# A 2:4-pruned linear layer on one core: one weight copy split over two DMA queues, four products moved back, one magnitude pass halved

## The chip, the core and the metric

The kernel runs on one core of one Trainium2 chip. The metric is the device time of one execution in microseconds (us). The median of three runs is given; lower is better. A separate execution was recorded by the hardware profiler, and the profile below is of that one.

The engines that matter here are TensorE (PE in the profile; PEld is its weight load), VectorE (DVE), ScalarE (ACT) and SyncE (SP). SP and ACT also issue DMA transfers, each on a queue of its own; the transfers of both are carried by the same 16 DMA engines.

## The reference, cut to what matters

```python
B, S, D = 16, 512, 1024              # x: B,S,D   w: D,D   b: D   all bf16
wg = w.reshape(D // 4, 4, D)         # groups of four neighbouring rows
mag = jnp.abs(wg)
order = jnp.argsort(mag, 1)
thr = jnp.take_along_axis(mag, order[:, 2:3, :], 1)
mask = mag >= thr                    # the two largest of each four stay
wp = (wg * mask).reshape(D, D)
return jnp.einsum("bsd,df->bsf", x, wp) + b
```

So the kernel prunes a 1024 x 1024 weight, multiplies 8192 tokens by it and adds a bias.

## The kernel before, in words

The 8192 tokens are 64 tiles of 128. From tile 9 on, the work is a plain loop (line 301): for each tile, 16 matmuls of 512 columns against the pruned weight in natural row order (`wp_nat`, one tensor for each half h of the columns), with the transposed x brought by DMA transposes in batches (`issue_batch`, line 219: tiles 9 to 11, then 12 to 15, then eight at a time). VectorE adds the bias out of PSUM, and ACT's queue stores.

The first nine tiles are computed while the weight is still arriving and being pruned. That part is a list of tokens written out by hand, `FRONT`; each engine does its share of it in the list's order. `w` comes in packed order: the four rows of a group lie in one partition. It is cut in seven pieces, numbered as in `pieces`: 0 to 3 are the first 512 contraction rows (g = 0) in four steps of 256 columns, 4 and 5 are columns 0 to 511 of the second 512 rows (g = 1), and 6 is the last 512 columns of g = 1. The tokens:

- `A.i` takes the magnitudes of piece i (line 122 on VectorE for pieces 0 and 1, line 120 on ScalarE for the others); `P.i` finds the threshold, the mask, and multiplies the weight by it in place (lines 133 to 143, VectorE).
- `W`, `w`: warm-up matmuls on zeros. `T.t` transposes the first half of x tile t on TensorE (line 160), `C.t` copies it out on ScalarE (line 165).
- `M.i.t` multiplies tile t by piece i, four matmuls (line 179), one for each of m = 0 to 3; `X.q.t` does so for a whole quarter of 512 columns; `N.i.t.m` does the one matmul m.
- `V.h.t` copies the partial sum of g = 0 to SBUF on ScalarE (line 193), and `O.h.t` adds the partial sum of g = 1 to it on VectorE (line 197).
- `U.g.h.c0.c1` moves a pruned piece to natural rows (line 150): four DMAs, j = 0 to 3, each writes one block of 128 rows of `wp_nat`. The products with g = 1 (pieces 4 to 6) read these blocks, m being the block j.
- `L.k` issues the k-th batch of transposes of x (line 219).

`U` and `L` are issued by SP, in the order of the list; a queue's next issue waits until the one before it is issued. ACT's own loads, two of them, come at the very start (the second half of piece 0's rows and x tiles 2 and 3); after the last `V` it issues nothing until the stores. Every DMA reports its landing on one of eight semaphores, used in turn, and before one is used again the issuing queue waits for the landing of the DMA that had it last.

Around the places that are changed, the list before runs like this:

```
A.0 P.0 W ... T.0 T.1 C.0 T.2 T.3 C.1 w T.4 T.5 C.2 w M.0.0 A.1 C.3 M.0.1 P.1 C.4 T.6 T.7 C.5
M.0.2 M.0.3 C.6 M.0.4 A.2 M.0.5 M.0.6 C.7 P.2 M.1.0 A.3 M.0.7 M.1.1 A.4 M.1.2 M.1.3 V.0.0
...
P.6 U.1.1.0.512 U.0.1.0.512 L.0 L.1 L.2 V.1.2 X.1.8 ... V.1.8 M.4.6 ... M.5.7 O.0.4 X.2.8 O.0.5
N.6.0.0 N.6.0.1 O.0.6 N.6.0.2 N.6.1.0 N.6.1.1 O.0.7 N.6.0.3 N.6.1.2 N.6.1.3 M.6.2 ...
```

`U.1.1.0.512` is piece 6; its four blocks are called j0 to j3 below. `N.6.0.0` is the first product that reads j0, `N.6.0.1` j1, `N.6.0.2` j2 and `N.6.0.3` j3.

Of the kernel before, what the change touches and what calls it, by code (L numbers as in the profile page):

```python
# [10 lines left out]
def kernel(  # L11
# [7 lines left out]
    nc = tc.nc  # L19
    P = 128  # L20
    bf16 = mybir.dt.bfloat16
    fp32 = mybir.dt.float32
    u16 = mybir.dt.uint16
    Alu = mybir.AluOpType
    Act = mybir.ActivationFunctionType
    K = tc.keep_in_program_order
# [36 lines left out]
    w_gh = {(g, h): const.tile([P, 4, FH], bf16, name=f"w_{g}_{h}") for g in range(2) for h in range(2)}  # L63

    def w_of(i):
        g, c0, c1 = pieces[i]
        return w_gh[(g, c0 // FH)][:, :, c0 % FH:c0 % FH + c1 - c0]
# [39 lines left out]
    def warm(n):  # L107
        K(nc.tensor.matmul(bank[7][:, :n], lhsT=zeros[:, :P], rhs=zeros[:, :n], start=True, stop=True))  # L108
# [3 lines left out]
    def abs_piece(i, on_act):  # L112
        g, c0, c1 = pieces[i]
        n = c1 - c0
        if n <= 256:
            mag = mags_pool.tile([P, 4, n], bf16, name="mag")[:]
        else:
            mag = const.tile([P, 4, n], bf16, name=f"mag_{i}")[:]
        if on_act:
            K(nc.scalar.activation(mag, w_of(i), Act.Abs))  # L120
        else:
            K(nc.vector.tensor_single_scalar(
                mag.bitcast(u16), w_of(i).bitcast(u16), 0x7FFF, op=Alu.bitwise_and))
        mags[i] = mag

    def prep_piece(i):
        g, c0, c1 = pieces[i]
        n = c1 - c0
        mag = mags.pop(i)
        magv = mag.rearrange("p (a j) f -> p a j f", j=2)  # L130
        hi = tmp.tile([P, 2, FH], bf16, name="hi")[:, :, :n]
        lo = tmp.tile([P, 2, FH], bf16, name="lo")[:, :, :n]
        K(nc.vector.tensor_tensor(hi, magv[:, :, 0, :], magv[:, :, 1, :], op=Alu.max))  # L133
        K(nc.vector.tensor_tensor(lo, magv[:, :, 0, :], magv[:, :, 1, :], op=Alu.min))  # L134
        t1 = tmp.tile([P, FH], bf16, name="t1")[:, :n]
        t2 = tmp.tile([P, FH], bf16, name="t2")[:, :n]
        K(nc.vector.tensor_tensor(t1, hi[:, 0, :], hi[:, 1, :], op=Alu.min))
        K(nc.vector.tensor_tensor(t2, lo[:, 0, :], lo[:, 1, :], op=Alu.max))
        thr = tmp.tile([P, FH], bf16, name="thr")[:, :n]
        K(nc.vector.tensor_tensor(thr, t1, t2, op=Alu.max))  # L140
        mask = tmp.tile([P, 4, FH], bf16, name="mask")[:, :, :n]
        K(nc.vector.tensor_tensor(mask, mag, thr[:, None, :].to_broadcast([P, 4, n]), op=Alu.is_ge))  # L142
        K(nc.vector.tensor_tensor(w_of(i), w_of(i), mask, op=Alu.mult))  # L143

    wp_nat = [const.tile([P, KT, FH], bf16, name=f"wp_nat{h}") for h in range(2)]


    def unpack(g, h, c0, c1):
        for j in range(4):
            K(nc.sync.dma_start(wp_nat[h][:, 4 * g + j, c0:c1], w_gh[(g, h)][32 * j:32 * (j + 1), :, c0:c1]))  # L150

    xT = {}
    own = {}
# [1 line left out]
    def transpose_half(t):  # L155
        own[(0, t)] = next_bank()
        xv = xh[t].rearrange("p (q m) -> p m q", m=4)
        dst = bank[own[(0, t)]][:].bitcast(bf16)[:, :4 * P].rearrange("p (m q) -> p m q", m=4)
        for m in range(4):
            K(nc.tensor.transpose(dst[:, m, :], xv[:, m, :], ident[:]))  # L160

    def copy_half(t):
        xt = const.tile([P, 4, P], bf16, name=f"xT_{t}")
        src = bank[own[(0, t)]][:].bitcast(bf16)[:, :4 * P].rearrange("p (m q) -> p m q", m=4)
        K(nc.scalar.copy(xt[:], src))  # L165
        xT[t] = xt


    def mm_part(q, t, c0, c1, ms=range(4)):
        g, h = divmod(q, 2)  # L170
        if c0 == 0 and q > 0 and 0 in ms:
            own[(q, t)] = next_bank()
        dst = bank[own[(q, t)]][:, c0:c1]
        for m in ms:
            if g == 0:
                lhs, rhs = xT[t][:, m, :], w_gh[(0, h)][:, m, c0:c1]
            else:
                lhs, rhs = xg1[:, m, t * P:(t + 1) * P], wp_nat[h][:, 4 + m, c0:c1]
            K(nc.tensor.matmul(dst, lhsT=lhs, rhs=rhs, start=c0 == 0 and m == 0, stop=c1 == FH and m == 3))  # L179
# [11 lines left out]
    def to_stage(h, t):  # L191
        stage[(h, t)] = const.tile([P, FH], fp32, name=f"stage{h}_{t}")
        K(nc.scalar.copy(stage[(h, t)][:], bank[own[(h, t)]][:]))  # L193

    def add_stage(h, t):
        st = stage[(h, t)][:]
        K(nc.vector.tensor_tensor(st, bank[own[(2 + h, t)]][:], st, op=Alu.add))  # L197

    def add_bias(h, t):
        f = slice(h * FH, (h + 1) * FH)  # L200
        K(nc.vector.tensor_tensor(get_o(t)[:, f], stage.pop((h, t))[:], bias_sb[:, f], op=Alu.add))  # L201
        if (1 - h, t) not in stage:
            store(t)
# [10 lines left out]
    def issue_batch(t0, nb):  # L214
        if nb < 8:
            xt = const.tile([P, KT, nb * P], bf16, name=f"xTs{t0}")
        else:
            xt = xtb.tile([P, KT, nb * P], bf16, name="xTb")
        K(nc.sync.dma_start_transpose(out=xt[:], in_=xf[t0 * P:(t0 + nb) * P, :]))
        for j in range(nb):  # L220
            xN[t0 + j] = xt[:, :, j * P:(j + 1) * P]
# [8 lines left out]

    FRONT = """
        A.0 P.0 W W W W W W W W w w T.0 T.1 C.0 T.2 T.3 C.1 w T.4 T.5 C.2 w M.0.0 A.1 C.3 M.0.1 P.1 C.4 T.6 T.7 C.5
        M.0.2 M.0.3 C.6 M.0.4 A.2 M.0.5 M.0.6 C.7 P.2 M.1.0 A.3 M.0.7 M.1.1 A.4 M.1.2 M.1.3 V.0.0 M.1.4 M.1.5 V.0.1
        P.3 M.1.6 V.0.2 M.1.7 V.0.3 T.8 M.2.0 C.8 M.2.1 M.2.2 V.0.4 X.0.8 V.0.5 P.4 U.1.0.0.256 V.0.6 M.2.3 M.2.4
        A.5 M.2.5 M.3.0 V.0.7 M.3.1 V.0.8 M.2.6 P.5 U.1.0.256.512 U.0.0.0.512 M.3.2 V.1.0 M.2.7 A.6 M.3.3 M.3.4
        M.3.5 M.3.6 V.1.1 M.3.7 P.6 U.1.1.0.512 U.0.1.0.512 L.0 L.1 L.2 V.1.2 X.1.8 V.1.3 M.4.0 V.1.4 M.4.1 V.1.5
        M.4.2 M.4.3 V.1.6 M.4.4 V.1.7 M.4.5 N.5.0.0 V.1.8 M.4.6 N.5.0.1 N.5.0.2 M.4.7 N.5.0.3 M.5.1 O.0.0 M.5.2
        O.0.1 M.5.3 M.5.4 O.0.2 M.5.5 M.5.6 O.0.3 M.5.7 O.0.4 X.2.8 O.0.5 N.6.0.0 N.6.0.1 O.0.6 N.6.0.2 N.6.1.0
        N.6.1.1 O.0.7 N.6.0.3 N.6.1.2 N.6.1.3 M.6.2 O.0.8 O.1.0 M.6.3 O.1.1 M.6.4 O.1.2 M.6.5 O.1.3 M.6.6 O.1.4
        O.1.5 M.6.7 O.1.6 X.3.8 O.1.7 O.1.8  # L240
    """
    for tok in FRONT.split():
        k, *n = tok.split(".")
        n = [int(c) for c in n]
        if k in "MN":
            g, c0, c1 = pieces[n[0]]
            h = c0 // FH
            mm_part(2 * g + h, n[1], c0 - h * FH, c1 - h * FH, n[2:] or range(4))
        elif k in "Ww":
            warm(FH if k == "W" else P)  # L250
        elif k == "A":
            abs_piece(n[0], n[0] >= 2)
        elif k == "P":
            prep_piece(n[0])
        elif k == "T":
            transpose_half(n[0])
        elif k == "C":
            copy_half(n[0])
        elif k == "X":
            mm_part(n[0], n[1], 0, FH)  # L260
        elif k == "V":
            to_stage(*n)
        elif k == "O":
            add_stage(*n)
        elif k == "B":
            add_bias(*n)
        elif k == "U":
            unpack(*n)
        elif k == "L":
            issue_batch(*batches[n[0]])  # L270
    later = [(h, t) for t in range(T) for h in range(2) if (h, t) in stage]
# [19 lines left out]
    for bi, (t0, nb) in enumerate(batches):  # L291
        if bi >= 1 and bi + 2 < len(batches):
            issue_batch(*batches[bi + 2])
        for t in range(t0, t0 + nb):
# [11 lines left out]
            j = (t - T) % 2  # L306
# [36 lines left out]
```

## Time and profile before

| what | value |
|---|---|
| time, median of 3 runs | 235.18 us (235.05 to 235.23) |
| time of the profiled execution | 234.39 us |
| its span, first to last instruction | 232.6 us |
| TensorE clock granted over the span | 1.000 |
| TensorE busy | 226.6 us, 1163 matmuls recorded |
| VectorE busy | 116.0 us |
| ScalarE busy | 20.7 us |

The profiled execution's time is its span and 1.8 us around it. The rows of the profile are start, duration, engine, line, operation, output<-inputs and count, and in square brackets how long the engine was idle before, with what ended that. A "q" behind an engine's name is its issuing side. A matmul's shown duration is its latency: neighbours overlap, and their cost is the distance between two starts, 0.216 us for 512 columns, 0.109 for 256 and 0.056 for 128. A few matmul records are missing from the trace.

### The profile page before, as it was taken

To read this page: it belongs to the slowest core of one execution; us is meant where nothing else is said; L and a number is where in the kernel's file an instruction comes from. 1 tells how busy PE (TensorE), PEld (TensorE's weight loads), DVE (VectorE), ACT (ScalarE), POOL (GpSimd) and SP (SyncE) were. 2 spreads that over 40 slices of the span, in tenths; PEclk is the share of its full clock that TensorE was granted. 3 is DMA by queue.
4 is the path that set the end of the run, shared out by engine and by line. 5 is a ranking of instruction groups with operands and counts; after the bars stand their busy time and mean duration, and the time that the engine had idled before them with its cause. 6 is when DMAs were issued, how large, how long until landed. Compare 5 with 4: busy or idle time off the path is not lost.

```text
span 232.6 us, 2804 instructions
## 1 busy us (share of the span) xinstructions
PE 226.6 (97%) x1163; PEld 113.8 (49%) x1184; DVE 116.0 (50%) x200; ACT 20.7 (9%) x34; POOL 0.7 (0%) x6
## 2 busy tenths in 40 slices
PE   7999999999999999999999999999999999999995
PEld 3788854444444444444444444444444444444443
DVE  4999898994484234334334324424424423433433
ACT  3999300000000000000000000000000000000000
POOL 1000000000000000000000000000000000000000
PEclk9999999999999999999999999999999999999999
DMA  6993589999998522971259510893229922221132
GB/s 191 353 245 71 124 198 259 194 268 97 293 319 261 208 90 93 269 227 45 90 150 290 191 74 20 217 303 116 90 90 179 272 93 90 90 90 46 47 135 90
DMA packets 77084, 38.19 MB, mean 164 GB/s; under 512 B 62352, under 2 KB 68880, under 8 KB 77072
## 3 DMA queue, kind: packets, MB, share of 16 engines
q1 hardware_dynamic: 67728, 20.91, 42.9%
q10 hardware_dynamic: 9344, 17.11, 20.7%
q8 instruction: 9, 0.15, 0.3%
q14 instruction: 3, 0.02, 0.0%
HBM read 3.54 MB, written 16.78 MB: 87 GB/s over the span
## 4 chain that ended last, share of the span: by engine, by line
PE 94%; DMA 3%; issue 1%; DVE 0%; SPq 0%; DVEq 0%
PE bank L301 80%; PE bank L179 12%; DMA xh<-in_x_dram 2%; PE bank L276 1%; DMA wp_nat<-w 1%; PE bank L160 1%; DVE stage L197 0%; SPq L79 0%; SPq L71 0%; DVE o_sb L286 0%; PE bank L108 0%; SPq L150 0%; DVEq L197 0%
## 5 line engine op out<-in xcount | busy, mean ns | idle before, releaser
L301 PE MATMUL bank<-wp_nat,xTb 128*128 128x512 bf16 x738 | 161.7, 379 | 0.8
L207 DVE TENSOR_TENSOR o_pair<-bank,bias_sb 128x512 bf16<-128x512 f32 x108 | 69.3, 685 | 100.3 <-PE bank L301 95.8
L301 PEld LDWEIGHTS <-xTb 128*128 128x128 bf16 x752 | 73.5, 98 | 88.8
L301 PE MATMUL bank<-wp_nat,xTs 128*128 128x512 bf16 x109 | 24.0, 379 | 0.1
L301 PEld LDWEIGHTS <-xTs 128*128 128x128 bf16 x112 | 11.0, 98 | 13.2
L179 PE MATMUL bank<-w,xT 128*128 128x256 bf16 (+1 forms) x134 | 16.1, 277 | 0.1
L179 PE MATMUL bank<-wp_nat,xg 128*128 128x256 bf16 (+1 forms) x103 | 16.0, 313 | 0.1
L201 DVE TENSOR_TENSOR o_sb<-stage,bias_sb 128x512 bf16<-128x512 f32 x18 | 11.5, 684 | 6.4 <-DMA out_dram<-o_sb 6.4
L179 PEld LDWEIGHTS <-xT 128*128 128x128 bf16 x136 | 13.2, 98 | 2.2
L179 PEld LDWEIGHTS <-xg 128*128 128x128 bf16 x104 | 10.2, 98 | 5.8 <-issue 0.6
L197 DVE TENSOR_TENSOR stage<-bank,stage 128x512 f32<-128x512 f32 x18 | 11.6, 685 | 1.9 <-PE bank L179 1.9
L193 ACT COPY stage<-bank 128x512 f32<-128x512 f32 x18 | 9.2, 614 | 0.0
L120 ACT ACTIVATE mag<-w 128x1024 bf16<-128x1024 bf16 (+1 forms) x5 | 6.1, 1233 | 0.4 <-DMA w<-in_w_dram 0.4
L142 DVE TENSOR_TENSOR mask<-mag,thr 128x1024 bf16<-128x1024 bf16 (+1 forms) x7 | 5.4, 769 | 0.2
L143 DVE TENSOR_TENSOR w<-w,mask 128x1024 bf16<-128x1024 bf16 (+1 forms) x7 | 5.4, 768 | 0.2
L165 ACT COPY xT<-bank 128x512 bf16<-128x512 bf16 x9 | 4.8, 602 | 2.4 <-PE bank L160 2.3
L108 PE MATMUL bank<-zeros 128*128 128x512 bf16 (+1 forms) x12 | 3.7, 456 | 1.2 <-DVE zeros L101 1.2
L276 PE MATMUL bank<-wp_nat,xTb 128*128 128x128 bf16 (+2 forms) x31 | 3.6, 269 | 0.1
L160 PE MATMUL bank<-ident,xh 128*128 128x128 bf16 x36 | 2.8, 222 | 0.7 <-DMA xh<-in_x_dram 0.7
L133 DVE TENSOR_TENSOR hi<-mag 128x512 bf16<-128x512 bf16 (+1 forms) x7 | 3.2, 459 | 0.1
L134 DVE TENSOR_TENSOR lo<-mag 128x512 bf16<-128x512 bf16 (+1 forms) x7 | 3.2, 455 | 0.0
L276 PEld LDWEIGHTS <-xTb 128*128 128x128 bf16 x32 | 2.5, 98 | 1.3
(16 smaller groups left out, 15.3 us busy)
## 6 DMA issues: line engine op xcount, KB each, us to landing
out_dram<-o_pair ACTq DMA_DIRECT2D x26, 512.0 KB, 3.6
out_dram<-o_sb ACTq DMA_DIRECT2D x9, 256.0 KB, 6.3
w<-in_w_dram SPq DMA_DIRECT2D x3, 512.0 KB, 6.5
wp_nat<-w SPq DMA_DIRECT2D x12, 128.0 KB, 2.9
xh<-in_x_dram SPq DMA_DIRECT2D x3, 256.0 KB, 4.6
wp_nat<-w SPq DMA_DIRECT2D x8, 64.0 KB, 2.1
out_dram<-o_pair ACTq DMA_DIRECT2D x2, 256.0 KB, 2.0
xh<-in_x_dram ACTq DMA_DIRECT2D x1, 256.0 KB, 4.2
```

The costliest lines, as they stand in the source:

```text
L120: K(nc.scalar.activation(mag, w_of(i), Act.Abs))
L142: K(nc.vector.tensor_tensor(mask, mag, thr[:, None, :].to_broadcast([P, 4, n]), op=Alu.is_ge))
L143: K(nc.vector.tensor_tensor(w_of(i), w_of(i), mask, op=Alu.mult))
L160: K(nc.tensor.transpose(dst[:, m, :], xv[:, m, :], ident[:]))
L165: K(nc.scalar.copy(xt[:], src))
L179: K(nc.tensor.matmul(dst, lhsT=lhs, rhs=rhs, start=c0 == 0 and m == 0, stop=c1 == FH and m == 3))
L193: K(nc.scalar.copy(stage[(h, t)][:], bank[own[(h, t)]][:]))
L197: K(nc.vector.tensor_tensor(st, bank[own[(2 + h, t)]][:], st, op=Alu.add))
L201: K(nc.vector.tensor_tensor(get_o(t)[:, f], stage.pop((h, t))[:], bias_sb[:, f], op=Alu.add))
L207: K(nc.vector.tensor_tensor(o_sb[:, f], bank[bk][:], bias_sb[:, f], op=Alu.add))
L276: K(nc.tensor.matmul(bank[bk][:, :c1 - c0], lhsT=xN[t][:, kt, :], rhs=wp_nat[h][:, kt, c0:c1], start=kt == 0, stop=kt == KT - 1))
L301: K(nc.tensor.matmul(bank[bks[h]][:], lhsT=xN[t][:, kt, :], rhs=wp_nat[h][:, kt, :], start=kt == 0, stop=kt == KT - 1))
```

## The change

Three things are changed.

1. `abs_piece`: for piece 0 the magnitude pass on VectorE is two instructions, rows m = 0, 1 and rows m = 2, 3, where it was one for all four. The two halves of this piece are loaded by two DMAs, the first on SP's queue and the second on ACT's.
2. `FRONT`: `M.0.7`, the eighth tile's products with piece 0, comes after `M.1.2`; it came after `M.1.0`.
3. `unpack` is given the queue and a range of j. Of piece 6, j0 and j1 stay at their place on SP's queue; j2 and j3 become a token `Z`, issued on ACT's queue, in the list behind `V.1.8`. What followed them on SP's queue (`U.0.1.0.512`, `L.0`, `L.1`, `L.2`) follows j1 directly.

```diff
-            K(nc.vector.tensor_single_scalar(
-                mag.bitcast(u16), w_of(i).bitcast(u16), 0x7FFF, op=Alu.bitwise_and))
+            for ms in (slice(0, 2), slice(2, 4)) if i == 0 else (slice(0, 4),):
+                K(nc.vector.tensor_single_scalar(
+                    mag[:, ms].bitcast(u16), w_of(i)[:, ms].bitcast(u16), 0x7FFF, op=Alu.bitwise_and))
...
-    def unpack(g, h, c0, c1):
-        for j in range(4):
-            K(nc.sync.dma_start(wp_nat[h][:, 4 * g + j, c0:c1], w_gh[(g, h)][32 * j:32 * (j + 1), :, c0:c1]))
+    def unpack(eng, g, h, c0, c1, ja=0, jb=4):
+        for j in range(ja, jb):
+            K(eng.dma_start(wp_nat[h][:, 4 * g + j, c0:c1], w_gh[(g, h)][32 * j:32 * (j + 1), :, c0:c1]))
...
-        M.0.2 M.0.3 C.6 M.0.4 A.2 M.0.5 M.0.6 C.7 P.2 M.1.0 A.3 M.0.7 M.1.1 A.4 M.1.2 M.1.3 V.0.0 M.1.4 M.1.5 V.0.1
+        M.0.2 M.0.3 C.6 M.0.4 A.2 M.0.5 M.0.6 C.7 P.2 M.1.0 A.3 M.1.1 A.4 M.1.2 M.0.7 M.1.3 V.0.0 M.1.4 M.1.5 V.0.1
...
-        M.3.5 M.3.6 V.1.1 M.3.7 P.6 U.1.1.0.512 U.0.1.0.512 L.0 L.1 L.2 V.1.2 X.1.8 V.1.3 M.4.0 V.1.4 M.4.1 V.1.5
-        M.4.2 M.4.3 V.1.6 M.4.4 V.1.7 M.4.5 N.5.0.0 V.1.8 M.4.6 N.5.0.1 N.5.0.2 M.4.7 N.5.0.3 M.5.1 O.0.0 M.5.2
+        M.3.5 M.3.6 V.1.1 M.3.7 P.6 U.1.1.0.512.0.2 U.0.1.0.512 L.0 L.1 L.2 V.1.2 X.1.8 V.1.3 M.4.0 V.1.4 M.4.1
+        V.1.5 M.4.2 M.4.3 V.1.6 M.4.4 V.1.7 M.4.5 N.5.0.0 V.1.8 Z.1.1.0.512.2.4 M.4.6 N.5.0.1 N.5.0.2 M.4.7 N.5.0.3
...
-        elif k == "U":
-            unpack(*n)
+        elif k in "UZ":
+            unpack(nc.sync if k == "U" else nc.scalar, *n)
```

More of the change, by code (lines that the diff above doesn't have):

```diff
@@ L232 @@
         A.0 P.0 W W W W W W W W w w T.0 T.1 C.0 T.2 T.3 C.1 w T.4 T.5 C.2 w M.0.0 A.1 C.3 M.0.1 P.1 C.4 T.6 T.7 C.5
-        M.0.2 M.0.3 C.6 M.0.4 A.2 M.0.5 M.0.6 C.7 P.2 M.1.0 A.3 M.0.7 M.1.1 A.4 M.1.2 M.1.3 V.0.0 M.1.4 M.1.5 V.0.1
+        M.0.2 M.0.3 C.6 M.0.4 A.2 M.0.5 M.0.6 C.7 P.2 M.1.0 A.3 M.1.1 A.4 M.1.2 M.0.7 M.1.3 V.0.0 M.1.4 M.1.5 V.0.1
         P.3 M.1.6 V.0.2 M.1.7 V.0.3 T.8 M.2.0 C.8 M.2.1 M.2.2 V.0.4 X.0.8 V.0.5 P.4 U.1.0.0.256 V.0.6 M.2.3 M.2.4
         A.5 M.2.5 M.3.0 V.0.7 M.3.1 V.0.8 M.2.6 P.5 U.1.0.256.512 U.0.0.0.512 M.3.2 V.1.0 M.2.7 A.6 M.3.3 M.3.4
-        M.3.5 M.3.6 V.1.1 M.3.7 P.6 U.1.1.0.512 U.0.1.0.512 L.0 L.1 L.2 V.1.2 X.1.8 V.1.3 M.4.0 V.1.4 M.4.1 V.1.5
-        M.4.2 M.4.3 V.1.6 M.4.4 V.1.7 M.4.5 N.5.0.0 V.1.8 M.4.6 N.5.0.1 N.5.0.2 M.4.7 N.5.0.3 M.5.1 O.0.0 M.5.2
-        O.0.1 M.5.3 M.5.4 O.0.2 M.5.5 M.5.6 O.0.3 M.5.7 O.0.4 X.2.8 O.0.5 N.6.0.0 N.6.0.1 O.0.6 N.6.0.2 N.6.1.0
-        N.6.1.1 O.0.7 N.6.0.3 N.6.1.2 N.6.1.3 M.6.2 O.0.8 O.1.0 M.6.3 O.1.1 M.6.4 O.1.2 M.6.5 O.1.3 M.6.6 O.1.4
-        O.1.5 M.6.7 O.1.6 X.3.8 O.1.7 O.1.8
+        M.3.5 M.3.6 V.1.1 M.3.7 P.6 U.1.1.0.512.0.2 U.0.1.0.512 L.0 L.1 L.2 V.1.2 X.1.8 V.1.3 M.4.0 V.1.4 M.4.1
+        V.1.5 M.4.2 M.4.3 V.1.6 M.4.4 V.1.7 M.4.5 N.5.0.0 V.1.8 Z.1.1.0.512.2.4 M.4.6 N.5.0.1 N.5.0.2 M.4.7 N.5.0.3
+        M.5.1 O.0.0 M.5.2 O.0.1 M.5.3 M.5.4 O.0.2 M.5.5 M.5.6 O.0.3 M.5.7 O.0.4 X.2.8 O.0.5 N.6.0.0 N.6.0.1 O.0.6
+        N.6.0.2 N.6.1.0 N.6.1.1 O.0.7 N.6.0.3 N.6.1.2 N.6.1.3 M.6.2 O.0.8 O.1.0 M.6.3 O.1.1 M.6.4 O.1.2 M.6.5 O.1.3
+        M.6.6 O.1.4 O.1.5 M.6.7 O.1.6 X.3.8 O.1.7 O.1.8
     """
```

## The prediction, as it was put on record

> **What bounds the kernel now.** I read the page first (busy times, chain by engine), then the chain in order of time, then the timelines of the stretches that the diff touches. All starts below are of the profiled execution.
>
> ```profile
> span 232.6 us, 2804 instructions
> ...
> PE 226.6 (97%) x1163; PEld 113.8 (49%) x1184; DVE 116.0 (50%) x200; ACT 20.7 (9%) x34; POOL 0.7 (0%) x6
> ...
> PE 94%; DMA 3%; issue 1%; DVE 0%; SPq 0%; DVEq 0%
> ```
>
> TensorE is busy for 97% of the span and makes 94% of the chain. The change removes no matmul, so it can only gain TensorE's idle time. Start to start of its matmuls, I find four waits after the first transposes: 0.37 us before 6.38, 0.09 before 6.99, 0.18 before 8.04, 0.03 before 10.73, and then nothing until 31.66. (Other long steps are missing records: two pitches of 0.216.) Two more come at 31.89 and 32.23, and none after that up to the last tile.
>
> ```profile
> 6.25 0.69 DVE L143 TENSOR_TENSOR w<-w,mask 128x1024 bf16<-128x1024 bf16 x1
> ...
> 6.85 0.22 PE L108 MATMUL bank<-zeros 128*128 128x128 bf16 x1
> ...
> 6.99 1.03 PE L179 MATMUL bank<-w,xT 128*128 128x256 bf16 x8
> ...
> 7.27 0.43 DVE L122 TENSOR_SCALAR mag<-w 128x1024 uint16<-128x1024 uint16 x1 [0.33 <-DMA w<-in_w_dram]
> ...
> 8.04 0.48 PEld L160 LDWEIGHTS <-xh 128*128 128x128 bf16 x8 [0.29 <-DMA xh<-in_x_dram]
> ...
> 9.98 0.69 DVE L143 TENSOR_TENSOR w<-w,mask 128x1024 bf16<-128x1024 bf16 x1
> ...
> 10.48 0.57 ACT L165 COPY xT<-bank 128x512 bf16<-128x512 bf16 x1
> ```
>
> This is the timeline of the start. P.0 ends at 6.25 + 0.69 = 6.94 and releases M.0.0 at 6.99. T.6 then waits for x until 8.04, and A.1 for its weight until 7.27: both pinned by a DMA's landing.
>
> ```profile
> 28.56 3.29 DMA wp_nat<-w
> 31.85 0.04 issue
> 31.89 7.84 PE bank L179 x35
> ```
>
> ```profile
> 30.36 1.18 PEld L179 LDWEIGHTS <-xg 128*128 128x128 bf16 x7
> 31.89 0.10 PEld L179 LDWEIGHTS <-xg 128*128 128x128 bf16 x1 [0.35 <-issue]
> 32.23 0.10 PEld L179 LDWEIGHTS <-xg 128*128 128x128 bf16 x1 [0.24 <-issue]
> ```
>
> The chain goes through one DMA of piece 6: j1, issued at 28.56, lands at 31.85, and N.6.0.1 starts at 31.89. N.6.0.0 started at 31.44, so N.6.0.1 was due at 31.66: a wait of 0.24. N.6.0.2 is due at 32.11 and starts at 32.23, behind j2's landing at 32.19: 0.12. Together 0.36 us, 0.15% of the time. That is all that this profile offers the change's third part.
>
> **Part 1, the halved magnitudes.** The loads of piece 0's halves land at 3.29 (SP) and 3.52 (ACT); the one pass starts at 3.54, takes 0.43, and the next step starts at 4.00. No row shows a half pass. It is at least half of the whole, 0.21, and at most the whole, 0.43; two-input rows show 0.42 at 512 elements and 0.28 at 256, so the cost is part fixed: I take 0.29. The first half then runs from 3.31 to 3.60, and the second to about 3.85: 0.14 gained (0 to 0.22, none if the second costs as much as the whole). P.0 ends at 6.80. The warm-up matmul at 6.85 holds TensorE until 6.91, so M.0.0 gains 0.08. M.0.0 and M.0.1 end 0.08 sooner, and T.6 still waits for x until 8.04: worth nothing. If x landed early, the 0.08 would be lost again at M.1.0, which stands at 10.73 behind P.1's end (9.98 + 0.69 = 10.67), and P.1 starts from the landing at 7.27. I take 0.
>
> **Part 2, M.0.7.** Same four matmuls, later. M.0.7 starts at 11.16, and C.7, which it needs, ends at 10.48 + 0.57 = 11.05: it does not wait now, with 0.11 to spare. Behind M.1.1 and M.1.2 it starts 8 x 0.109 = 0.87 later, with 0.98 to spare. M.1.1 and M.1.2 come 0.44 earlier and need only P.1 and copies that are long done. Worth 0 here; up to 0.87 in an execution in which C.7 is late (it stands behind A.2 on ACT, which waits for its weight until 9.52). Nothing is lost: the first V waits behind A.4 until 12.85.
>
> **Part 3, two queues.** On SP, 20 DMAs of line 150 follow each other, then the transposes:
>
> ```profile
> 19.29 13.79 SPq L150 DMA_DIRECT2D wp_nat<-w  x20
> 33.13 7.33 SPq L219 DMA_TRANSPOSE xTs<-in_x_dram  x2
> 40.50 28.76 SPq L219 DMA_TRANSPOSE xTb<-in_x_dram  x2
> ```
>
> ```profile
> wp_nat<-w SPq DMA_DIRECT2D x12, 128.0 KB, 2.9
> ```
>
> They go out every 0.65 us: j0 at 27.96, j1 at 28.56, j2 at 29.21, j3 at 29.86. P.6 is done at 26.97, but SP is still busy with the transfer before until 27.86. ACT's last V ends at 25.29 and its first store goes at 41.69, so Z waits there for P.6 alone, nothing is queued behind it, and j2 goes out at 27.02 and j3 at about 27.6 (an issue took 0.50 on ACT at the start, 0.60 on SP here). With a landing 2.6 to 3.5 us after issue (the rows of this kind) they land between 29.6 and 31.2, before N.6.0.2 can ask: 0.12 gained. j0 and j1 keep their issue times, since what stands ahead of them on SP is unchanged. N.6.0.1 is free of its wait if j1 lands within 3.05 us (2.7 is common, it took 3.29); it keeps 0.24 at 3.29; and it gets worse by as much as j2 and j3 slow it. Ends: 0.36 gained with j1 quick; at the other, j1 later by all of Z's 256 KB at the 200 GB/s that the engines moved from 29 to 34, 1.28 us, less 0.12: 1.16 lost. I take the row itself, 3.29: between 28.5 and 29.5 the engines show a busy share of 0.87, so they have a little room, and from 27.5 to 28.0 they moved only a quarter of that rate, which Z can fill. Sum of part 3: **0.12 us gained.**
>
> What comes later: U.0.1 and the transposes go out 2 x 0.65 = 1.3 us sooner. The batch for tile 16 landed at 62.30 and was used at 63.74; TensorE did not wait for it, so this is worth 0 here.
>
> [...]
>
> **The sum.** 0 + 0 + 0.12. The profiled execution would take 234.39 - 0.12 = 234.27. The median of the runs is 0.79 above that execution; I cannot see where, carry it over as it is, and get 235.18 - 0.12 = 235.06, so 235.05. A difference under about 0.2% (0.47 us) cannot be told from no change.
>
> **The rivals.**
>
> - *The 0.79 us of the usual executions lie in waits that this change shortens.* If C.7 is late by 0.4 more than here, M.0.7 waits 0.3 now and not after; if the batch for tile 16 is late by over its 1.44, the 1.3 us of earlier issue pay for it; and N.6's 0.36 goes. That is 0.5 to 0.8 faster: 234.4 to 234.7. For it: these margins (0.11, 1.44) are thin beside landings that spread by 0.9 us. Against: the profile shows neither wait.
> - *The two queues share the DMA engines, and j0 and j1 pay.* TensorE needs j0 and j1 first, and Z's bytes are ahead of them. From the point where j1 lands 0.59 us later than now (32.44), the loss passes 0.47: with 0.6 to 1.28 us of delay, 235.7 to 236.35. For it: busy share 0.87. Against: Z starts nearly one microsecond ahead, in a half-idle stretch.
> - *Z does not go out early.* A DMA that uses a semaphore again waits for the one eight before it: the store at 62.37 goes right after the batch's landing at 62.30. In the source, Z's j2 is the eighth behind j1. Were they counted so, Z would go at 31.9, land at 34.6, and N.6.0.2 would wait 2.4: 237.6. Against: in the trace semaphores are handed out in the order in which work gets ready (ACT's first load has the first, though SP's stands first in the source); by that order the ones Z takes were free at 26.2.
>
> **How the numbers follow.** The forecast, anything from the full 0.36 gained to 0.45 lost (234.8 to 235.6), gets 0.45; the late waits 0.32; the shared engines 0.20; the late Z 0.03. So faster 0.32, same 0.45, slower 0.23. The range reaches into both neighbours, 234.4 to 235.9, and leaves out the late Z, the upper half of the shared engines and a little of the first rival.
>
> **What would show it.** After: the first magnitude row near 3.3 and P.0's end near 6.80, with T.6 still at its landing; M.0.7 without a wait; two ACT issues of line 150 near 27.0; the transposes near 31.8; N.6.0.2 right behind N.6.0.1. It is wrong if j1 lands after 32.4, if ACT issues Z after 28, or if TensorE's waits before 11 us shrink by over 0.2 us.

## The result, and the profile after

The kernel after takes 235.93 us (median of 19 runs, 234.17 to 236.68); the kernel before, 234.83 (19 runs, 234.32 to 236.08). The ratio is 1.0038, with a 95% interval of 1.0021 to 1.0055: it is slower, by about 0.9 us by the ratio and 1.1 by the medians. The forecast was 0.12 us faster.

The first view is TensorE's weight loads around N.6 in the profile of after (start, duration, engine, line, operation, inputs, count, and the idle time ahead with what ended it).

```profile
32.00 0.31 PEld L180 LDWEIGHTS <-xg 128*128 128x128 bf16 x2
33.95 0.33 PEld L180 LDWEIGHTS <-xg 128*128 128x128 bf16 x3 [1.64 <-DMA wp_nat<-w]
```

The last matmul of X.2.8 starts at 32.43, so N.6.0.0 is due at 32.65; it starts at 33.95. That is one wait of 1.31 us, where before had 0.24 and 0.12. It is for j0, which lands at 33.91. Behind it N.6.0.1 and N.6.0.2 follow without a gap. The chain of the same profile names something else:

```profile
32.06 1.89 DVE stage L198 x3
33.95 0.00 issue
33.95 7.94 PE bank L180 x36
```

A wait for several semaphores is put down to the one that came last. VectorE's addition ended at 33.95 too, but what N.6.0.0 needs of VectorE is the bank of an earlier tile, which was read by 30.3. The weight load's row, and the landing, name the real cause. Where they disagree, ask which data the instruction reads.

Then the issues of `unpack` in the stretch of piece 6 (median landing at the end of the row), and the two queues in order of time:

```profile
wp_nat<-w SPq DMA_DIRECT2D x4, 128.0 KB, 4.1
wp_nat<-w ACTq DMA_DIRECT2D x2, 128.0 KB, 4.3
```

```profile
28.21 1.33 ACTq L151 DMA_DIRECT2D wp_nat<-w  x2
```

ACT issues Z at 28.21, when P.6 ends at 28.18, as forecast. But the transfers that took 2.9 us on one queue now take 4.1 to 4.3: j0 goes out at 28.99 and lands 4.92 later.

This execution had a second difference. x tiles 6 and 7 landed at 9.21 and not at 8.00, so everything from there to N.6 stands 1.2 us later than in the profile of before. The profiled execution took 236.53 us, 0.6 above the median of the runs. The span is 234.7 against 232.6: 1.2 from there, 0.95 from N.6. From the start of tile 9 on, the two profiles agree within 0.02 us: tile 16 starts 24.17 later in both, and the end comes 168.83 after that. Whatever the change does, it has done by tile 9.

### The profile page after: what moved, and what is told of

It reads as the page before. It is cut to its first block, busy times and chain, and to the rows that moved or that the text cites. A ratio compares the mean times of both kernels' runs of the same rounds, so it can differ in the third digit from the quotient of the medians.

```text
span 234.7 us, 2826 instructions
## 1 busy us (share of the span) xinstructions
PE 228.4 (97%) x1184; PEld 114.2 (49%) x1184; DVE 116.4 (50%) x201; ACT 20.8 (9%) x34; POOL 0.7 (0%) x6
## 4 chain that ended last, share of the span: by engine, by line
PE 94%; DMA 3%; DVE 1%; SPq 1%; issue 0%; DVEq 0%
PE bank L302 79%; PE bank L180 13%; DMA xh<-in_x_dram 3%; PE bank L277 1%; DVE stage L198 1%; SPq L71 0%; SPq L79 0%; PE bank L161 0%; DVE o_sb L287 0%; DVEq L198 0%
## 5 line engine op out<-in xcount | busy, mean ns | idle before, releaser
L302 PEld LDWEIGHTS <-xTb 128*128 128x128 bf16 x752 | 73.6, 98 | 88.7
L108 PE MATMUL bank<-zeros 128*128 128x512 bf16 (+1 forms) x12 | 4.2, 509 | 1.2 <-DVE zeros L101 1.2
L161 PEld LDWEIGHTS <-xh 128*128 128x128 bf16 x36 | 2.6, 122 | 1.9 <-DMA xh<-in_x_dram 1.8
```

Of the source, the lines that this page charges most:

```text
L302: K(nc.tensor.matmul(bank[bks[h]][:], lhsT=xN[t][:, kt, :], rhs=wp_nat[h][:, kt, :], start=kt == 0, stop=kt == KT - 1))
```

## The experiments

Each ratio below is to the kernel before, run again beside that group of experiments, with its 95% interval in brackets.

**Which part it is.** The first kernel is before with part 3 alone (`unpack` as in part 3, here and wherever a kernel below splits a piece); the second is after without part 3.

```diff
-P.6 U.1.1.0.512 U.0.1.0.512 ... V.1.8 M.4.6
+P.6 U.1.1.0.512.0.2 U.0.1.0.512 ... V.1.8 Z.1.1.0.512.2.4 M.4.6     (all of the first kernel)
```

> The kernel before with part 3 alone: j2 and j3 of piece 6 on ACT's queue, nothing else changed. Theory A (the two queues share the DMA engines, and j0, which TensorE needs first, lands late behind the bytes of j2 and j3): the whole loss is here, 0.5 to 1.3 us over before, with one TensorE wait of about 1.3 us ahead of N.6.0.0 and j0 landing 4 to 5 us after its issue. Theory B (the loss sits in the first 12 us, with the halved magnitudes or the moved products): within 0.3 us of before, j0 landing under 3.3 us after its issue.

> The kernel after without part 3: halved magnitudes and moved products, all four blocks of piece 6 on SP's queue. Theory A: within 0.3 us of before, the waits at N.6.0.1 and N.6.0.2 together 0.2 to 0.6 us. Theory B: 0.5 to 1.3 us slower than before, with longer TensorE waits before 12 us.

Part 3 alone: 235.68 us, ratio 1.0052 (1.0032 to 1.0072). Without part 3: 234.51, ratio 0.9996 (0.9981 to 1.0011). In the first, j0 lands 4.76 us after its issue and N.6.0.0 waits 1.44; in the second, j0 and j1 land after 2.66 and 2.92, and the only wait is 0.17 at N.6.0.2. The loss is all in part 3, and theory B falls. x tiles 6 and 7 landed at 8.08 and 7.93 in these two. The chain of part 3 alone names the transfer, j0, itself:

```profile
28.14 4.76 DMA wp_nat<-w
32.89 0.05 issue
32.94 7.94 PE bank L179 x36
```

The halved magnitudes do what the forecast said. In the kernel without part 3:

```profile
3.30 0.50 DVE L123 TENSOR_SCALAR mag<-w 128x512 uint16<-128x512 uint16 x2 [2.17 <-DMA w<-in_w_dram]
3.83 0.43 DVE L134 TENSOR_TENSOR hi<-mag 128x512 bf16<-128x512 bf16 x1
```

A half takes 0.29, and the second half runs from 3.51 to the next step at 3.83: 0.32 where the whole took 0.46, so 0.14 is gained, and A.1 still starts at 7.25.

**Bytes, or their order?** Next, the same two queues with j0 and j1 on ACT's; and one queue, with two blocks of U.0.0 moved behind piece 6.

```diff
-P.6 U.1.1.0.512.0.2 ... V.1.8 Z.1.1.0.512.2.4
+P.6 U.1.1.0.512.2.4 ... V.1.8 Z.1.1.0.512.0.2                       (exchange, from part 3 alone)
...
-U.1.0.256.512 U.0.0.0.512 ... P.6 U.1.1.0.512 U.0.1.0.512
+U.1.0.256.512 U.0.0.0.512.0.2 ... P.6 U.1.1.0.512 U.0.0.0.512.2.4 U.0.1.0.512     (from before)
```

> Part 3 the other way round: j0 and j1 on ACT's queue, j2 and j3 on SP's. Theory A (the engines move some 200 GB/s whatever the number of queues, and what is queued first lands first): j0 lands 3.8 us after its issue as Z's j2 did, about when it is due, j1 1.5 us later, so one wait of 0.6 to 1.0 us at N.6.0.1; 0.2 to 0.6 us slower than before, faster than part 3 alone. Rival A2 (only the order matters, the bytes do not): no wait at all, 0.3 us faster than before.

> The kernel before with one queue, but the last two blocks of U.0.0 put behind piece 6 on SP, so that SP is free when P.6 ends: j0 goes out 0.9 us sooner, with two blocks less ahead of it. Theory A: j0 to j3 land 2.6 to 3.3 us after issue, all before they are due, both waits of N.6 are gone, 0.3 to 0.4 us faster than before. If something other than the bytes ahead holds piece 6 (its issue, P.6's end), the waits stay and the time is that of before within 0.2 us.

The exchange: 234.39 us, ratio 0.9993 (0.9981 to 1.0005), and no wait at N.6 at all. Theory A, as I had it, falls. It expected the same 256 KB more among the same transfers to cost 0.6 to 1.0 us, but here everything landed within 2.8 to 3.6 us, also j2 and j3, which come last. Rival A2 (only the order matters) fits this run; the turned exchange below decides against it. Piece 6 ahead: 234.08 us, ratio 0.9979 (0.9968 to 0.9989), no wait at N.6 either; this one came as expected. TensorE's weight loads across N.6, in the exchange and then with piece 6 ahead, show no idle time:

```profile
30.53 3.77 PEld L179 LDWEIGHTS <-xg 128*128 128x128 bf16 x19
```

```profile
30.54 3.88 PEld L179 LDWEIGHTS <-xg 128*128 128x128 bf16 x19
```

The rates tell it. These are windows of 28.5 to 31 us; the last column is GB/s, the one before it the DMA engines' busy share. First before, then part 3 alone, then the exchange:

```profile
28.50:31.00 2.50, 2.46 (x22) 2.06 (x21) 2.50 (x5) 0.00 (x0) 0.00 (x0) 1.00 0.86 202
```

```profile
28.50:31.00 2.50, 2.50 (x24) 2.11 (x22) 2.50 (x6) 0.00 (x0) 0.00 (x0) 1.00 0.94 171
```

```profile
28.50:31.00 2.50, 2.50 (x25) 2.15 (x23) 2.50 (x5) 0.00 (x0) 0.00 (x0) 1.00 0.94 261
```

With two queues the engines are equally busy, 0.94, and move 171 GB/s in one case and 261 in the other; one queue moves 202. So a busy share of 0.94 does not say how much an engine moves. What differs is which blocks run beside each other. Block j is read from partitions 32j to 32j + 31. When Z starts, SP is issuing the last blocks of U.0.0, j2 and j3: partitions 64 to 127. Part 3 puts j2 and j3 beside them, the same half; the exchange puts j0 and j1, the other half. That is theory A'. In part 3 alone j0 itself is read from the other half, but it stands behind U.0.0's last two blocks in SP's queue: the second of them lands at 31.88 and j0 at 32.89, and in the profiles of before and after the transfers of `unpack` landed on each queue in the order of their issue (before, U.0.0's last block and j0 to j3: 29.94, 30.76, 31.85, 32.19 and 32.59).

**The half of the partitions.** Turning the order of U.0.0's blocks exchanges the cases, without moving piece 6:

```diff
-U.1.0.256.512 U.0.0.0.512
+U.1.0.256.512 U.0.0.0.512.2.4 U.0.0.0.512.0.2     (once in part 3 alone, once in the exchange)
```

> Part 3 alone, with U.0.0's blocks issued in the order j2, j3, j0, j1, so that the blocks beside j2 and j3 on ACT's queue are read from partitions 0 to 63 and not from 64 to 127. Theory A' (two transfers that read the same half of the partitions at once slow each other; from different halves they do not): the engines move some 250 GB/s between 28.5 and 31 instead of 170, j0 lands under 3.6 us after its issue, no or little wait at N.6.0.0, 0.9 us or more faster than part 3 alone and within 0.4 us of before. Theory A (bytes ahead alone): as part 3 alone, a wait of 1.3 to 1.5 us, 0.5 to 1.3 us slower than before.

> j0 and j1 on ACT's queue, j2 and j3 on SP's, with U.0.0's blocks in the order j2, j3, j0, j1: now the blocks that run beside each other are all read from partitions 0 to 63. Theory A': the slow case comes back although the first rows are on the early queue: j0 or j1 lands over 4 us after its issue, the engines move under 190 GB/s between 28.5 and 31, a TensorE wait of 0.3 to 1.2 us, slower than the same without the turn by 0.3 us or more. Theory A: no difference from the same without the turn, no wait at N.6.

Windows of the same stretch, part 3 turned and then the exchange turned:

```profile
28.50:31.00 2.50, 2.50 (x24) 2.15 (x23) 2.50 (x5) 0.00 (x0) 0.00 (x0) 1.00 0.89 240
```

```profile
28.50:31.00 2.50, 2.45 (x23) 2.05 (x22) 2.50 (x5) 0.00 (x0) 0.00 (x0) 1.00 0.94 179
```

The rates change sides: 171 becomes 240, and 261 becomes 179. Part 3 turned takes 235.19 us, ratio 1.0018 (1.0004 to 1.0032), 0.8 us less than unturned by the two ratios, whose intervals meet at 1.0032; the exchange turned takes 235.22, ratio 1.0011 (0.9991 to 1.0031), with a wait of 0.97 at N.6.0.1 for j1, which ACT issued at 27.61 and which landed 4.93 later. Its time is not apart from the unturned one's beyond the intervals; its landings, rate and wait are. It has the order of queues of the exchange and waits all the same, so A2 falls. Part 3 turned still waits 0.81 and 0.13, where little or none was expected. There j0 landed 3.40 after its issue, as expected, but went out late, at 28.99: SP spent 1.72 us on an issue at 26.21 (see the end). The transfers that N.6 waited for, in part 3 turned and then in the exchange turned:

```profile
28.99 3.40 DMA wp_nat<-w
```

```profile
27.61 4.93 DMA wp_nat<-w
```

**The copies by themselves.** This kernel leaves out the linear layer and only copies, so that its output is not the reference's.

```python
phases = (((0, 1, 2, 3), ()), ((0, 0, 1, 1), (2, 2, 3, 3)), ((2, 2, 3, 3), (2, 2, 3, 3)),
          ((2, 3, 2, 3), (3, 2, 3, 2)), ((0, 0, 1, 1), (1, 1, 0, 0)),
          ((0, 1, 2, 3), (2, 3, 0, 1)), ((2, 2, 3, 3), ()))        # blocks j on SP, on ACT
```

> No linear layer: only copies of the kind of line 150 (32 partitions with four rows each, to 128 rows, 128 KB), four on each queue, in seven stretches one after the other, nothing beside them; the output is not that of the reference. SP alone; SP from blocks 0, 1 with ACT from 2, 3; both from 2, 3 with equal blocks; both from 2, 3 with unequal blocks; both from 0, 1 with unequal blocks; SP 0 to 3 with ACT 2, 3, 0, 1; SP alone from 2, 3. Theory A': eight copies from two halves take little longer than four on one queue (last landing 4.5 to 5.5 us after the first issue), eight from one half some 1.3 to 2 us longer. Theory A: all four stretches of eight on two queues take the same within 0.3 us. If equal blocks alone are slow, the limit is the partition and not the half.

Windows inside the seven stretches of one execution, in that order (this kernel uses no TensorE; the columns are length, VectorE, GpSimd, clock, DMA share, GB/s):

```profile
5.80:8.30 2.50, 0.85 (x2) 0.00 (x0) 1.00 0.81 191
12.50:15.50 3.00, 1.56 (x4) 0.00 (x0) 1.00 0.95 280
20.50:25.00 4.50, 1.70 (x4) 0.00 (x0) 1.00 0.96 179
30.00:34.50 4.50, 1.83 (x5) 0.00 (x0) 1.00 0.97 187
39.50:44.00 4.50, 1.86 (x5) 0.00 (x0) 1.00 0.97 186
48.50:52.50 4.00, 1.54 (x4) 0.00 (x0) 1.00 0.91 246
57.20:59.50 2.30, 0.85 (x2) 0.00 (x0) 1.00 0.85 183
```

From the first issue to the last landing the stretches take 4.63, 5.86, 7.71, 7.54, 7.46, 6.42 and 4.64 us: a little longer from two halves than I expected, and 1.6 to 1.9 more from one. One queue moves 191 GB/s from all four blocks and 183 from one half alone, near the 202 of the kernel before, where 128 KB were issued every 0.65 us. Two queues that read from two halves move 280, and 246 where both change halves midway. Two that read from one half move 179 to 187, with equal blocks and with unequal ones, in the upper half and in the lower: no more than one queue, and the median landing of each queue is 4.4 to 4.8 us after issue, against 2.7 with one queue. In these copies it is the half that counts (280 against 179 to 187), not the partition (179 with equal blocks, 187 and 186 with unequal ones). Why two transfers from one half slow each other, these runs do not show.

**The rest.** Piece 6 ahead together with parts 1 and 2; the kernel after with the exchange alone; and the kernel after once more.

> Piece 6 ahead of the last two blocks of U.0.0 on SP, one queue, together with the halved magnitudes and the moved products. If those two parts are worth nothing, as the run without part 3 says: the time of piece 6 ahead alone within 0.25 us, 0.3 to 0.6 us faster than before. If they are worth something once the later waits are gone: 0.7 us or more faster than before.

> The kernel after with one thing exchanged: j0 and j1 go on ACT's queue at Z's place, j2 and j3 stay on SP's. Theory A': ACT's blocks are then read from the other half of the partitions than U.0.0's last two on SP, the engines move about 250 GB/s, no wait at N.6, 0.7 to 1.2 us faster than the kernel after and not slower than before (0 to 0.4 us faster). Theory A: still a wait of 0.5 us or more, 0.2 to 0.6 us slower than before.

> The kernel after, unchanged, for a second profile. In the first one x tiles 6 and 7 landed at 9.21, 1.2 us later than before. If that belongs to one execution: they land near 8.0 here, as in the runs with part 3 alone and without part 3, the span is near 233.6 and the wait at N.6.0.0 again 1.2 to 1.5 us. If the change does it: they land after 9 again.

Piece 6 ahead with both other parts: 234.00 us, ratio 0.9971 (0.9955 to 0.9987), the fastest of all, but not apart from piece 6 ahead alone (0.9979). After with the exchange: 234.39 us, ratio 0.9987 (0.9971 to 1.0002), about 1.35 us faster than after by the two ratios of that session, whose intervals lie apart, and not told from before. The rate from 28.5 to 31 us was 239 GB/s, about as expected, but its profile shows a wait of 0.50 at N.6.0.2: an SP issue of 2.04 us at 26.24 sent j2 out at 29.03.

After again: 235.84 us, ratio 1.0045 (1.0026 to 1.0065), the wait 1.73 at N.6.0.0 and 0.13 behind it. x tiles 6 and 7 landed at 8.61, neither of the two values I had expected. In the nine other profiles they landed between 7.79 and 8.28, also where the instructions up to there are the same, as in after with the exchange. Why both profiles of after were late there stays open. Both profiled executions took 0.6 us more than the median of their runs; with part 3 alone, landing at 8.08, the ratio was 1.0052, so the loss does not need it.

## Why the prediction was wrong, point by point

- **What bounds the kernel, and where it can gain.** Right. From the start of tile 9 to the end, all eleven profiles of the layer agree within 0.02 us; all differences lie in TensorE's waits before it. The two waits at N.6 are worth what the profile showed: piece 6 ahead removes them, and the ratio of 0.9979 is 0.49 us, with an interval of 0.26 to 0.75, for a sum of 0.36.
- **Part 1, nothing.** Right, with its working: half a pass 0.29, 0.14 gained, covered by the landings behind it.
- **Part 2, nothing.** Right as far as it can be told: parts 1 and 2 together have the ratio 0.9996. The late C.7 that the forecast named does occur: in two of the six profiles without part 2, the exchange and part 3 turned, M.0.7 waits 0.17 and 0.40 us for it. In the five with part 2 there is no such wait.
- **Part 3, 0.12 gained.** Wrong. Z went out when forecast: at 27.08 with part 3 alone, and in the profile of after at 28.21, later than the 28 that the forecast had set only by the late start of 1.21. The step that failed is "I take the row itself, 3.29 ... they have a little room": j1's landing, and j0's, which I gave no delay at all. With part 3 alone j0 landed 4.76 us after its issue, not 2.80, and cost one wait of 1.44; j1 landed at 33.09, later than the 32.4 that the forecast had set. What the runs showed in its place is that j2 and j3 were read from the same half of the partitions as the blocks that SP had in flight: together the two queues moved 171 GB/s, where one moved 202. I took 3.29 from a row of one queue, and read room out of a busy share below 1 and a rate of 200 GB/s. But 200 was the pace of the issues, 128 KB every 0.65 us, and not a limit of the engines, which moved 261 in the exchange; and the busy share said nothing of what a second queue would add: at 0.94 the two queues moved 171 in one case and 261 in the other.
- **"j0 and j1 keep their issue times", and the transposes go out "2 x 0.65 = 1.3 us sooner".** Wrong too. With part 3 alone j0 and j1 went out 0.2 and 0.5 us later than before, their issues took 0.90 and 1.60 us, and the transposes went out at 33.32, not 31.8.
- **The second rival** was the right side, with a mechanism that does not suffice; that its 235.7 to 236.35 holds the 235.93 is in part luck. It said that Z's bytes stand ahead of j0 and j1 and gave 0.6 to 1.28 us of delay; in the profile of after j0 landed at 33.91, which is 32.70 without the late start of 1.21, against 30.76 before: 1.9 later. If bytes alone counted, the exchange would have cost as much, and it cost nothing.
- **The first rival**, that the 0.79 us of the first three runs over the profiled execution hid waits: it does not hold as a whole. Its late C.7 occurs, as said, but parts 1 and 2 together changed nothing that can be told; its late batch for tile 16 occurs in no profile. Over 19 runs before's median is 234.83, and 0.79 was part of a spread of 1.8 us.
- **The third rival**, Z held by a semaphore: it did not happen; in the profile of after Z went out 0.03 us after P.6's end.

## What to carry to other kernels

Before two transfers are put side by side on two queues, look at which partitions they read: here two from one half of the partitions moved 171 GB/s together, less than the 202 of one queue, and two from opposite halves moved 261. The faster rate by itself gained no time that can be told here (ratios 0.9993 and 0.9987). Where a transfer is late because its queue is busy, moving less urgent work behind it on the same queue cost nothing here and gained 0.2% (ratio 0.9979). The rate that equalled the pace of the issues (202 GB/s, at 128 KB every 0.65 us) was no measure of what the engines had left: with a second queue that read from the other half they moved 261.

## What the runs showed of the hardware that was not expected

- The half of the partitions, as above: 280 GB/s from two halves, 179 to 187 from one, with the engines' busy share at 0.95 to 0.97 in both.
- While two queues read from one half, the issues themselves were longer: 1.0 to 1.45 us in the copies alone from the fourth issue on, where an issue of one queue alone took 0.54 to 0.62. From two halves they took up to 0.90, and once 1.44 where both queues change halves midway. With part 3 alone the issues of j0 and j1 took 0.90 and 1.60 us, where in the kernel before they took 0.56 and 0.61, and the transposes behind them on SP's queue went out at 33.32, where the forecast had 31.8.
- In eight of the eleven profiles of the layer one SP issue near 26 us took 1.07 to 2.04 us and not 0.60. In each profile a 16 KB packet of the instruction queue is in flight in that stretch, and in all ten in which SP then went on issuing, one issue ended 0.24 to 0.42 us after that packet did (before: the packet from 25.93 to 26.95, the issue from 25.96 to 27.22). That the one holds the other is argued from this, not tested. Two of the experiments show 0.50 and 0.94 us of wait at N.6 behind such an issue.
